# A gated network's second output product: four products per period against a seven-product scheme over six periods

## The chip, the cores and the metric

One core of one Trainium2 chip runs the whole kernel. The metric is the device time of one execution in microseconds (us); a kernel's time is the median of several runs. All inputs and outputs are float32.

## What is computed

```python
qn = q / (norm(q, axis=1) + 1e-6); kn = k / (norm(k, axis=1) + 1e-6)
a = softmax(kn.T @ qn / tau)              # 256 x 256, channels by channels
x = v @ a                                 # 6016 tokens x 256
xn = x / sqrt(mean(x*x) + 1e-6) * rms_g   # first gated layer
x = (silu(xn @ w_gate) * (xn @ w_val)) @ w_out
out = (sigmoid(x @ w_gate2) * (x @ w_val2)) @ w_out2   # second gated layer, d_ff = 1536
```

## The kernel before

Every operand of a matmul is held as a high and a low part (h and l, float32r), and each product is three matmuls, `mm3` (L104): high by high, high by low, low by high. Activations lie transposed: 256 channels are two chunks of 128 partitions, tokens are the columns. The 47 tiles of 128 tokens form 12 blocks, and two blocks one of six pairs; a pair has two halves of 512 columns (pair 2, which comes last in the second layer, has halves of 448). The 1536 hidden channels are 12 groups f of 128.

A head computes the attention and x. Then the first two pairs of layer one run block by block (`plain_gv`, `plain_h`, `out_mm`), while the weights of both layers are converted in steps that the loop pumps (`conversion`, L123): seven operands of 128 x 128 for gate and value and two output weights per f, split in high and low. Those of layer one stay in SBUF, those of layer two go to DRAM (`w2d`, L213) and are loaded once, f by f, into the buffers of layer one's weights during layer two's first pair (L850).

The rest is a stream of periods, one per (layer, pair, f), 48 of layer one and 72 of layer two. `period` (L491) is written out by hand, and every engine executes its instructions in that order. For gate and value it uses a scheme of seven products (`product`, L484) in place of eight on the two halves and two channel chunks of a pair: Z, B, then the fourth product of the previous period (T4), T2 into Z, B21 into A, T3 into Z, S4 into B; ScalarE and VectorE copy and add between them. The banks "g" (Z, B) and "v" (A, D) have two buffers each. In the same period the previous period's hidden values of both halves are finished (sigmoid on g1, `v1 = v1 * g1`, `v0 = v0 * sg0`) and split into hh and hl (L526, L527, L541, L542), and four output products (`out_mm`, L455) of the period before that add into four PSUM banks, y0, y1, at0, at1: two behind the A product, two at the end. After 12 periods the four banks are copied out and stored (`evacuate`, L468). `slots` holds per period what else is placed at its points "early", "ACT", "DVE", "end": the load of the next pair's operands, three sums on POOL (and a fourth later), and their splits. POOL does nothing else in layer two; all DMAs are issued from SP.

After the last period only the rest of its hidden values, four output products and the copies are left.

## Time and profile before

| | us |
|---|---|
| median of 3 runs | 1215.25 (1211.85 to 1217.26) |
| the profiled execution | 1211.54 |
| its span | 1209.8 |
| TensorE busy | 1179.6 (5398 matmuls) |
| VectorE / ScalarE / POOL busy | 781.7 / 792.6 / 180.2 |

Busy time is the union of an engine's rows; the rows of matmuls and of ScalarE and VectorE instructions overlap, so a row's duration is longer than the distance at which the next one can start. The first 100 us are the attention, the weights are converted up to about 300 us, the stream of layer one ends and that of layer two begins at about 655 us.

### The profile page before, as it was taken

Reading aid. Unit: us, or ns where it says so; the run is one execution under the profiler, and the core shown is the slowest. Engines: PE = TensorE matmul, PEld = TensorE weight load, DVE = VectorE, ACT = ScalarE, POOL = GpSimd, SP = SyncE. Lnnn points to the kernel's source line nnn. Section 1 sums busy time; section 2 is a strip of 40 time slices with the busy share of each in tenths; the row PEclk is TensorE's granted clock in tenths of the full one; section 3 lists DMA queues with packets and bytes.
Section 4 is the critical chain, followed back from the end, with each engine's and each line's share of the span. In section 5 each row is a group of like instructions: output and inputs, shape, how many; then the busy total and the mean of one; then the engine's idle time right before and its main releaser. Section 6 shows DMA issues by size and latency. Waiting matters only on the chain.

```text
span 1209.8 us, 14740 instructions
## 1 busy us (share of the span) xinstructions
PE 1179.6 (98%) x5398; PEld 987.9 (82%) x5398; DVE 781.7 (65%) x1166; ACT 792.6 (66%) x1459; POOL 180.2 (15%) x207
## 2 busy tenths in 40 slices
PE   8898989999999999999999999999999999999997
PEld 7786767788899888888888788888888888888997
DVE  6898888886556556556556556556555565565554
ACT  7766667775466666666666666666666666666664
POOL 0133665553200100100100100100100100100000
PEclk9999999999999999999999999999999999999999
DMA  9662335765300200200344400200200200100000
GB/s 345 242 231 105 122 107 188 269 223 211 112 1 1 66 1 1 70 1 1 130 162 162 156 1 1 70 1 1 70 1 1 70 1 1 66 1 1 35 1 31
DMA packets 42473, 98.48 MB, mean 81 GB/s; under 512 B 4768, under 2 KB 14496, under 8 KB 42400
## 3 DMA queue, kind: packets, MB, share of 16 engines
q1 hardware_dynamic: 42256, 97.41, 23.0%
q8 instruction: 42, 0.69, 0.2%
q14 instruction: 31, 0.25, 0.1%
q10 hardware_dynamic: 144, 0.13, 0.0%
HBM read 64.36 MB, written 33.16 MB: 81 GB/s over the span
## 4 chain that ended last, share of the span: by engine, by line
PE 79%; DVE 1%; ACT 1%; issue 0%; POOL 0%; ACTq 0%; DVEq 0%
PE g L105 12%; PE g L107 12%; PE g L106 12%; PE v L105 5%; PE v L106 5%; PE v L107 5%; PE at L106 5%; PE at L107 5%; PE at L105 5%; PE y L105 5%; PE y L106 5%; PE y L107 5%; DVE hl L527 0%; DVE v L521 0%; ACT hh L526 0%
## 5 line engine op out<-in xcount | busy, mean ns | idle before, releaser
L520 ACT ACTIVATE g<-g 128x512 f32<-128x512 f32 (+1 forms) x120 | 74.6, 621 | 158.9 <-DVE g L558 158.9
L556 DVE TENSOR_TENSOR v<-g,e 128x512 f32<-128x512 f32 (+1 forms) x120 | 81.4, 678 | 128.6 <-ACT v L554 128.6
L521 DVE TENSOR_TENSOR v<-v,g 128x512 f32<-128x512 f32 (+1 forms) x120 | 84.8, 707 | 81.9 <-ACT g L520 81.9
L527 DVE TENSOR_TENSOR hl<-v,hh 128x512 fp32r<-128x512 f32 (+1 forms) x120 | 83.3, 694 | 81.1 <-ACT hh L526 81.1
L542 DVE TENSOR_TENSOR hl<-v,hh 128x512 fp32r<-128x512 f32 (+1 forms) x120 | 81.4, 678 | 70.9 <-ACT hh L541 70.3
L554 ACT COPY v<-g 128x512 f32<-128x512 f32 (+1 forms) x120 | 67.2, 560 | 83.9 <-PE g L107 83.1
L105 PE MATMUL g<-xh,wh 128*128 128x512 f32 (+1 forms) x300 | 115.5, 385 | 0.2
L107 PE MATMUL g<-xh,wl 128*128 128x512 f32 (+1 forms) x300 | 115.3, 384 | 0.0
L106 PE MATMUL g<-xl,wh 128*128 128x512 f32 (+1 forms) x300 | 115.3, 384 | 0.0
L105 PE MATMUL at<-hh,wh 128*128 128x512 f32 (+1 forms) x288 | 111.2, 386 | 1.9 <-ACT hh L526 1.3
L105 PE MATMUL g<-qh,wh 128*128 128x512 f32 (+1 forms) x276 | 107.9, 391 | 5.2 <-ACT wh L182 5.2
L106 PE MATMUL at<-hl,wh 128*128 128x512 f32 (+1 forms) x288 | 111.5, 387 | 0.6 <-DVE hl L527 0.6
L107 PE MATMUL at<-hh,wl 128*128 128x512 f32 (+1 forms) x288 | 110.9, 385 | 0.0
L105 PE MATMUL y<-hh,wh 128*128 128x512 f32 (+1 forms) x288 | 110.9, 385 | 0.0
L106 PE MATMUL y<-hl,wh 128*128 128x512 f32 (+1 forms) x288 | 110.9, 385 | 0.0
L107 PE MATMUL y<-hh,wl 128*128 128x512 f32 (+1 forms) x288 | 110.9, 385 | 0.0
L107 PE MATMUL g<-qh,wl 128*128 128x512 f32 (+1 forms) x276 | 107.8, 390 | 2.2 <-DVE wl L190 2.2
L106 PE MATMUL g<-ql,wh 128*128 128x512 f32 (+1 forms) x276 | 107.0, 388 | 0.0
L105 PE MATMUL v<-qh,wh 128*128 128x512 f32 (+1 forms) x216 | 85.3, 395 | 3.9 <-DVE hl L451 3.6
L538 ACT COPY g<-g 128x512 f32<-128x512 f32 (+1 forms) x120 | 69.5, 579 | 28.3 <-PE g L107 28.0
L106 PE MATMUL v<-ql,wh 128*128 128x512 f32 (+1 forms) x216 | 83.9, 388 | 0.0
L107 PE MATMUL v<-qh,wl 128*128 128x512 f32 (+1 forms) x216 | 83.8, 388 | 0.0
(160 smaller groups left out, 2754.7 us busy)
## 6 DMA issues: line engine op xcount, KB each, us to landing
wraw<-in_w_dram SPq DMA_DIRECT2D x24, 768.0 KB, 4.9
w2d<-w2h SPq DMA_DIRECT2D x12, 576.0 KB, 2.8
w2d<-w2l SPq DMA_DIRECT2D x12, 576.0 KB, 3.2
wh<-w2d SPq DMA_DIRECT2D x12, 576.0 KB, 3.7
wl<-w2d SPq DMA_DIRECT2D x12, 576.0 KB, 4.7
vraw<-in_v_t_dram SPq DMA_DIRECT2D x11, 512.0 KB, 3.9
yd<-yo SPq DMA_DIRECT2D x20, 256.0 KB, 2.4
out_t_dram<-yo SPq DMA_DIRECT2D x20, 256.0 KB, 2.2
```

The source lines that it names most:

```text
L105: nc.tensor.matmul(ps, sh, mh, start=start, stop=False, skip_group_check=more)
L106: nc.tensor.matmul(ps, sh, ml, start=False, stop=False, skip_group_check=more)
L107: nc.tensor.matmul(ps, sl, mh, start=False, stop=stop, skip_group_check=more)
L520: nc.scalar.activation(out=pv["g1"], in_=pv["g1"], func=(AF.Silu, AF.Sigmoid)[pl])
L521: nc.vector.tensor_mul(pv["v1"], pv["v1"], pv["g1"])
L527: nc.vector.tensor_sub(hl1[:, :pw], pv["v1"], f32(hh1[:, :pw]))
L538: nc.scalar.copy(s["g1"], Z)
L542: nc.vector.tensor_sub(hl0[:, :pw], pv["v0"], f32(hh0[:, :pw]))
L554: nc.scalar.copy(D, Z)
L556: nc.vector.tensor_add(s["v1"], Z, e5)
```

## The change

Layer two's output product gets a scheme of seven products too. It pairs two groups f (hidden channels) and both output chunks, with the two halves of the columns; six periods' hidden values make three such pairs, a team, and a team has 7 kinds of operand times 3 pairs, 21 products. They run during the six periods that follow (`out_product`: one early in even periods, one behind the A product, two at the end), the last team's behind the last period. Two teams make a column pair. The sums of hidden values that the kinds need are made in place: a first sum and some third sums on VectorE, the others by DMAs from POOL's queue that add one SBUF tile into another (`more`), nine products ahead of their use. Signs are put into the gating multiplications (`gated`). The hidden tiles are kept in float32 in buffers of layer one's weights, and split when their product comes near (`split_high`, `split_low`). Results are gathered from four banks Z, B, A, D into four SBUF tiles after each kind (`gather`, called by `flush`) and stored from them.

Layer two's gate and value weights are now reloaded from DRAM for each period into three buffers (`gw_load`), and the output operands for each kind into four (`ow_load`). The output weights go to DRAM unsplit during conversion, and are loaded, split, summed and stored in layer one's stream (`out_load` to `sums_low`). The order of the operands in a weight tile changes; layer one's v1 gets one buffer instead of two; a_h and a_l move into a weight buffer. Not shown below: those moves, and the halved slices in `conversion`.

```diff
     NQ = 9
-    A11, A12, A21, A22, OUT, S1, S2, S4 = 0, 1, 2, 3, 4, 6, 7, 8
+    S1, S2, S4, A11, A12, A21, A22, OUT = range(8)
     S3 = A21
...
-    w2d = [dram.tile([P, 2, NQ, P], F32, name=f"w2d{f}") for f in range(NF)]
+    gd = [dram.tile([P, 2, NG, P], F32, name=f"gd{f}") for f in range(NF)]
+    rd = [dram.tile([P, 4, P], F32, name=f"rd{i}") for i in range(NF // 2)]
+    od = [dram.tile([P, 8, 2, NJ, P], F32, name=f"od{g}") for g in range(2)]
...
             t = w["t"]
+            if l:
+                nc.sync.dma_start(out=rd[f // 2][:, f % 2 * 2 : f % 2 * 2 + 2], in_=t[:, OUT:])
...
+    stream0 = [(0, p, f) for p in range(PLAIN, NP) for f in range(NF)]
+    stream1 = [(1, p, f) for p in (0, 1, 3, 4, 5, 2) for f in range(NF)]
+    stream = stream0 + stream1
+    HALF = NF // 2
+    teams = [(p, g) for _, p, f in stream1[::NF] for g in range(2)]
+    gw = {}
+    def gw_load(n):
+        if n < len(stream1):
+            gw[stream1[n]] = [wp.tile([P, NG, P], F32R, tag=f"w{e}{n % 3}", name="gw") for e in "hl"]
+            for e, t in enumerate(gw[stream1[n]]):
+                nc.sync.dma_start(out=f32(t), in_=gd[stream1[n][2]][:, e])
     def product(ps, it, i, a, start, stop=True):
         l, p, f = it
         h, lo = ops[l, p][i]
         w = hw[p]
-        mm3(ps[:, :w], wh[l, f][:, a], wl[l, f][:, a], h[:, :w], lo[:, :w], start, stop, not start)
-    def period(it, pv, outs, last=False):
+        ch, cl = gw[it] if l else (wh[0, f], wl[0, f])
+        mm3(ps[:, :w], ch[:, a], cl[:, a], h[:, :w], lo[:, :w], start, stop, not start)
+    odd = {}
+    def out_load(i):
+        odd["t"] = sp.tile([P, 4, P], F32, tag="t1", name="ot")
+        nc.sync.dma_start(out=odd["t"], in_=rd[i])
+    def out_store(i, h, lo, first):
+        g, j = divmod(i, NJ)
+        for e, t in enumerate((h, lo)):
+            nc.sync.dma_start(out=od[g][:, first : first + 4, e, j], in_=f32(t))
+    def out_split(i):
+        odd["h"] = sp.tile([P, 4, P], F32R, tag="t2", name="oh")
+        nc.scalar.copy(odd["h"], odd["t"])
+    def out_low(i):
+        lo = sp.tile([P, 4, P], F32R, tag="ol", name="ol")
+        nc.vector.tensor_sub(lo, odd["t"], f32(odd["h"]))
+        out_store(i, odd["h"], lo, 0)
+    def out_sums(i):
+        w11, w21, w12, w22 = (odd["t"][:, u] for u in range(4))
+        nc.gpsimd.tensor_add(w22, w21, w22)
+        nc.gpsimd.tensor_sub(w21, w11, w21)
+        nc.gpsimd.tensor_sub(w11, w22, w11)
+        nc.gpsimd.tensor_sub(w12, w11, w12)
+    def sums_low(i):
+        lo = sp.tile([P, 4, P], F32R, tag="ol", name="ol")
+        nc.vector.tensor_sub(lo, odd["t"], f32(odd["h"]))
+        out_store(i, odd["h"], lo, 4)
+    homes = [f"w{e}{f}" for f in range(5, NF - 1) for e in "hl"]
+    hs, xs = [], []
+    def h_tile():
+        hs.append(wp.tile([P, 2, 512], F32, tag=homes[len(hs) % len(homes)], name="hs"))
+        return hs[-1]
+    def gated(out, v, gate, negative):
+        if negative:
+            nc.vector.scalar_tensor_tensor(out=out, in0=v, scalar=-1.0, in1=gate, op0=ALU.mult, op1=ALU.mult)
+        else:
+            nc.vector.tensor_mul(out, v, gate)
+    def first_sum(n):
+        w = hw[stream1[n][1]]
+        xs.append(sp.tile([P, 512], F32, tag=f"t{len(xs) % NJ}", name="t"))
+        nc.vector.tensor_add(xs[-1][:, :w], hs[n][:, 0, :w], hs[n][:, 1, :w])
+    def third_sum(n):
+        w = hw[stream1[n][1]]
+        b, d = hs[n - 1][:, 1, :w], hs[n][:, 1, :w]
+        if n % HALF == HALF - 1:
+            nc.vector.tensor_add(b, b, d)
+        else:
+            more(b, d)
+    def more(to, t):
+        nc.gpsimd.dma_start(out=to, in_=t, accum_op=ALU.add)
+    KINDS = ("11", "S1", "12", "S2", "S4", "S3", "22")
+    PLACE = ("11", "21", "12", "22", "S2", "S3", "S4", "S1")
+    ow = deque()
+    ow_n = [0]
+    def ow_load():
+        i, k = divmod(ow_n[0], len(KINDS))
+        if i < len(teams):
+            tag = ("wh3", "wl3", "wh4", "wl4")[ow_n[0] % 4]
+            t = wp.tile([P, 2, NJ, P], F32R, tag=tag, name="ow")
+            nc.sync.dma_start(out=f32(t), in_=od[teams[i][1]][:, PLACE.index(KINDS[k])])
+            ow.append(t)
+        ow_n[0] += 1
+    job, kept = {}, {}
+    due, lows = deque(), deque()
+    LAST = len(KINDS) * NJ
+    def team_start(i):
+        p, g = teams[i]
+        w = hw[p]
+        if g == 0:
+            kept["r"] = [
+                t[:, e, :w] for t in (wp.tile([P, 2, 512], F32, tag=f"w{u}{NF - 1}", name="r") for u in "hl")
+                for e in range(2)
+            ]
+            kept["A"], kept["D"] = y_bank(1), at_bank(1)
+        n = HALF * i
+        job.clear()
+        job.update(
+            p=p, g=g, w=w, split=0, done=0, parts={},
+            x=NJ * i,
+            h=[[hs[n + 2 * j + u][:, e, :w] for u in range(2) for e in range(2)] for j in range(NJ)],
+            A=kept["A"][:, :w], D=kept["D"][:, :w], r=kept["r"],
+        )
+    def split_high(ahead):
+        while job and job["split"] < min(LAST, job["done"] + ahead):
+            i = job["split"]
+            k, j = divmod(i, NJ)
+            a, b, c, d = job["h"][j]
+            src = xs[job["x"] + j][:, : job["w"]] if KINDS[k] == "S1" else {"12": c, "S4": d, "S3": b}.get(KINDS[k], a)
+            h, lo = (hidden(t)[:, : job["w"]] for t in ("hh", "hl"))
+            nc.scalar.copy(h, src)
+            job["parts"][i] = h, lo
+            job["split"] += 1
+            lows.append((i, h, lo, src))
+    def split_low():
+        while lows:
+            i, h, lo, src = lows.popleft()
+            nc.vector.tensor_sub(lo, src, f32(h))
+            k, j = divmod(i, NJ)
+            a, b, c, d = job["h"][j]
+            if KINDS[k] in ("11", "S2"):
+                more(a, b if KINDS[k] == "11" else c)
+    def out_product():
+        if not job or job["done"] == LAST:
+            return
+        k, j = divmod(job["done"], NJ)
+        kind = KINDS[k]
+        w = job["w"]
+        if j == 0 and kind in ("11", "S1"):
+            name = "Z" if kind == "11" else "B"
+            job[name] = (y_bank if kind == "11" else at_bank)(0)[:, :w]
+        ps = job[{"12": "A", "22": "D", "S1": "B", "S4": "B"}.get(kind, "Z")]
+        start = j == 0 and (kind in ("11", "S1") or (job["g"] == 0 and kind in ("12", "22")))
+        mm3(ps, ow[0][:, 0, j], ow[0][:, 1, j], *job["parts"].pop(job["done"]), start, True, not start)
+        job["done"] += 1
+        if j == NJ - 1:
+            ow.popleft()
+            ow_load()
+            due.append(partial(gather, kind, dict(job)))
+    def send(v, c, e, t):
+        p, w = v["p"], v["w"]
+        nc.sync.dma_start(out=out_t[c * P : (c + 1) * P, p0[p] + e * w : p0[p] + (e + 1) * w], in_=t)
+    def minus(out, src):
+        nc.scalar.activation(out=out, in_=src, func=AF.Copy, scale=-1.0)
+    def gather(kind, v):
+        Z, B, A, D = (v.get(n) for n in "ZBAD")
+        r11, r12, r21, r22 = v["r"]
+        add, sub = nc.vector.tensor_add, nc.vector.tensor_sub
+        again = v["g"]
+        if kind in ("11", "S2", "S3"):
+            r = {"11": r11, "S2": r12, "S3": r21}[kind]
+            if again:
+                add(r, Z, r)
+            else:
+                nc.scalar.copy(r, Z)
+        if kind == "S1":
+            if again:
+                sub(r22, r22, B)
+            else:
+                minus(r22, B)
+        if kind == "S3":
+            add(r22, Z, r22)
+        if kind == "S4":
+            sub(r12, r12, B)
+        if again and kind in ("12", "22"):
+            r, ps = (r11, A) if kind == "12" else (r21, D)
+            sub(r, r, ps)
+        if again:
+            for k, c, e, r in (("12", 0, 0, r11), ("S4", 0, 1, r12), ("S3", 1, 1, r22), ("22", 1, 0, r21)):
+                if k == kind:
+                    send(v, c, e, r)
+    def flush():
+        while due:
+            due.popleft()()
+    def period(it, pv, n, outs=()):
...
             product(s["v0"], s["it"], T4, A22, False)
-            nc.vector.tensor_mul(s["v0"], s["v0"], s["sg0"])
+            gated(s["h"][:, 0, :w] if l else s["v0"], s["v0"], s["sg0"], l and f % 2)
+        def split(ahead):
+            if n1 >= 0:
+                split_high(ahead)
+                split_low()
+        def out(count):
+            for _ in range(count):
+                if outs:
+                    outs.popleft()()
+                elif n1 >= 0:
+                    out_product()
         if it:
             l, p, f = it
...
             pl, pp, pf = pv["it"]
             pw = hw[pp]
             nc.scalar.activation(out=pv["g1"], in_=pv["g1"], func=(AF.Silu, AF.Sigmoid)[pl])
-            nc.vector.tensor_mul(pv["v1"], pv["v1"], pv["g1"])
-        if it:
-            nc.scalar.copy(A, Z)
-        if pv:
+            gated(pv["v1"], pv["v1"], pv["g1"], pl and pf % 2 == 0)
+        flush()
+        if n1 > 0 and n1 % HALF == 0:
+            team_start(n1 // HALF - 1)
+        if n1 > 0 and pf % 2:
+            third_sum(n1 - 1)
+        split(2)
+        if not it:
+            while job["done"] < LAST:
+                split(3)
+                out_product()
+                flush()
+            return
+        nc.scalar.copy(A, Z)
+        if pv and pl == 0:
             hh1, hl1 = hidden("hh"), hidden("hl")
             nc.scalar.copy(hh1[:, :pw], pv["v1"])
             nc.vector.tensor_sub(hl1[:, :pw], pv["v1"], f32(hh1[:, :pw]))
             hid[pl, pp, 1, pf] = hh1, hl1
-            if not pv.get("done"):
-                fourth(pv)
+            fourth(pv)
+        e5 = sp.tile([P, 512], F32, tag="e5", name="e5")[:, :w]
+        if pv and pl:
+            nc.scalar.copy(e5, B)
+            if n1 > 0:
+                split_high(3)
+            fourth(pv)
+            gw_load(n1 + 2)
+            split_low()
+            if pf % 2 == 0:
+                first_sum(n1 - 1)
         at("early")
-        if it:
-            e5 = sp.tile([P, 512], F32, tag="e5", name="e5")[:, :w]
+        if not (pv and pl):
             nc.scalar.copy(e5, B)
-            product(Z, it, T2, S2, False)
-            product(A, it, B21, A12, False)
-            s["g1"] = sp2.tile([P, 512], F32, tag="g1", name="g1")[:, :w]
-            nc.scalar.copy(s["g1"], Z)
-        if pv:
+        else:
+            out(1 if n1 % 2 == 0 else 0)
+        product(Z, it, T2, S2, False)
+        product(A, it, B21, A12, False)
+        s["g1"] = sp2.tile([P, 512], F32, tag="g1", name="g1")[:, :w]
+        nc.scalar.copy(s["g1"], Z)
+        if pv and pl == 0:
             hh0, hl0 = hidden("hh"), hidden("hl")
             nc.scalar.copy(hh0[:, :pw], pv["v0"])
             nc.vector.tensor_sub(hl0[:, :pw], pv["v0"], f32(hh0[:, :pw]))
             hid[pl, pp, 0, pf] = hh0, hl0
-        if it:
-            s["sg0"] = ip2.tile([P, 512], F32, tag="sg", name="sg")[:, :w]
-            nc.scalar.activation(out=s["sg0"], in_=A, func=act)
-        for _ in range(2):
-            outs.popleft()()
-        at("ACT")
-        at("DVE")
-        if it:
-            product(Z, it, T3, S3, False)
-            D = s["v0"] = gv_bank("v")[:, :w]
-            nc.scalar.copy(D, Z)
-            s["v1"] = sp2.tile([P, 512], F32, tag="v1", name="v1")[:, :w]
-            nc.vector.tensor_add(s["v1"], Z, e5)
-            product(B, it, B22, S4, False)
-            nc.vector.tensor_add(s["g1"], s["g1"], B)
-        if last:
-            outs.popleft()()
+        flush()
+        if n1 % 2 == 0:
+            split(3)
+        if n1 >= 0:
+            out(2 if outs else 1)
+            at("DVE")
+        s["sg0"] = ip2.tile([P, 512], F32, tag="sg", name="sg")[:, :w]
+        nc.scalar.activation(out=s["sg0"], in_=A, func=act)
+        if n1 < 0:
+            out(2)
+            at("ACT")
+            at("DVE")
+        product(Z, it, T3, S3, False)
+        D = s["v0"] = gv_bank("v")[:, :w]
+        nc.scalar.copy(D, Z)
+        if l:
+            s["h"] = h_tile()
+            s["v1"] = s["h"][:, 1, :w]
+        else:
+            s["v1"] = sp.tile([P, 512], F32, tag="t0", name="v1")[:, :w]
+        nc.vector.tensor_add(s["v1"], Z, e5)
+        flush()
+        if n1 >= 0:
+            split_high(3)
+            at("ACT")
+        product(B, it, B22, S4, False)
+        nc.vector.tensor_add(s["g1"], s["g1"], B)
+        split_low()
+        if n == len(stream) - 1:
+            out(2)
             fourth(s)
-            s["done"] = True
-        while outs:
-            outs.popleft()()
+        else:
+            out(max(2, len(outs)))
         at("end")
         return s
...
-            s = period(it, pv, outs, n == len(stream) - 1)
+            if 6 <= n < 6 + 6 * NF // 2 and n % NF % 6 == 0:
+                i = n // 6 - 1
+                slots[0].setdefault("end", []).append(partial(out_load, i))
+                slots[1].setdefault("ACT", []).append(partial(out_split, i))
+                slots[1].setdefault("end", []).append(partial(out_low, i))
+                slots[2].setdefault("end", []).append(partial(out_sums, i))
+                slots[4].setdefault("ACT", []).append(partial(out_split, i))
+                slots[4].setdefault("end", []).append(partial(sums_low, i))
+            s = period(it, pv, n, outs)
             if pv and pv["it"][:2] == (0, NP - 1):
                 g = pv["it"][2]
-                for d, e, tag in ((wh, 0, "wh"), (wl, 1, "wl")):
-                    d[1, g] = wp.tile([P, NQ, P], F32R, tag=f"{tag}{g}", name=tag)
-                    nc.sync.dma_start(out=f32(d[1, g]), in_=w2d[g][:, e])
+                if g < 3:
+                    gw_load(g)
+                if g == 4:
+                    for _ in range(4):
+                        ow_load()
             pv = s
-            outs = [(l, p, e, f) for e in (1, 0)]
-        for e in range(2):
-            for c in range(KC):
-                evacuate(*stream[-1][:2], e, c, c, e == 1)
+            outs = [(*it[:2], e, it[2]) for e in (1, 0)] if it and it[0] == 0 else []
```

## Rows read from the trace of the kernel before

**Rows 1.** The page's head: span; busy time, share and instructions by engine.

```profile
span 1209.8 us, 14740 instructions
PE 1179.6 (98%) x5398; PEld 987.9 (82%) x5398; DVE 781.7 (65%) x1166; ACT 792.6 (66%) x1459; POOL 180.2 (15%) x207
```

**Rows 2.** Stretches: length, busy time (x count) of each engine, PEclk, DMA share, GB/s.

```profile
190.00:220.00 30.00, 27.63 (x116) 21.01 (x114) 26.58 (x34) 21.13 (x38) 15.43 (x21) 1.00 0.62 219
655.00:1200.00 545.00, 544.66 (x2441) 457.67 (x2440) 320.29 (x492) 354.93 (x641) 25.56 (x20) 1.00 0.09 30
```

**Rows 3.** Timeline, a period of layer two, 512 columns: start, duration, instruction, [idle before].

```profile
899.77 0.39 PE L107 MATMUL g<-xh,wl 128*128 128x512 f32 x1
900.00 0.39 PE L105 MATMUL g<-xh,wh 128*128 128x512 f32 x1
...
900.25 0.57 ACT L554 COPY v<-g 128x512 f32<-128x512 f32 x1 [0.59 <-PE g L107]
...
900.86 0.69 DVE L556 TENSOR_TENSOR v<-g,e 128x512 f32<-128x512 f32 x1 [0.88 <-ACT v L554]
...
901.46 0.68 DVE L558 TENSOR_TENSOR g<-g,g 128x512 f32<-128x512 f32 x1
...
902.04 0.39 PE L105 MATMUL g<-xh,wh 128*128 128x512 f32 x1
...
902.17 0.63 ACT L520 ACTIVATE g<-g 128x512 f32<-128x512 f32 x1 [1.35 <-DVE g L558]
...
904.96 0.59 ACT L538 COPY g<-g 128x512 f32<-128x512 f32 x1 [0.29 <-PE g L107]
...
905.55 0.59 ACT L541 CAST hh<-v 128x512 fp32r<-128x512 f32 x1
...
906.03 0.61 ACT L546 ACTIVATE sg<-v 128x512 f32<-128x512 f32 x1
...
907.73 0.57 ACT L554 COPY v<-g 128x512 f32<-128x512 f32 x1 [0.59 <-PE g L107]
```

**Rows 4.** Timeline, the end of the kernel, 448 columns.

```profile
1190.69 0.36 PE L105 MATMUL g<-zh,wh 128*128 128x448 f32 x1
...
1197.37 0.37 PE L105 MATMUL g<-zh,wh 128*128 128x448 f32 x1
...
1197.78 0.36 PE L107 MATMUL g<-zh,wl 128*128 128x448 f32 x1
...
1201.84 0.62 DVE L527 TENSOR_TENSOR hl<-v,hh 128x448 fp32r<-128x448 f32 x1 [0.63 <-ACT hh L526]
...
1202.38 0.62 DVE L542 TENSOR_TENSOR hl<-v,hh 128x448 fp32r<-128x448 f32 x1
1202.52 0.47 PE L106 MATMUL at<-hl,wh 128*128 128x448 f32 x1 [0.19 <-DVE hl L527]
...
1205.08 1.86 SPq L480 DMA_DIRECT2D out_t_dram<-yo  x4
1205.47 0.54 ACT L473 COPY yo<-at 128x448 f32<-128x448 f32 x1
```

**Rows 5.** DMA issues: tiles, queue, count, KB each, median us to landing.

```profile
wl<-w2d SPq DMA_DIRECT2D x12, 576.0 KB, 4.7
...
yd<-yo SPq DMA_DIRECT2D x20, 256.0 KB, 2.4
...
in<-in_q_dram SPq DMA_DIRECT2D x13, 384.0 KB, 6.1
```

**Rows 6.** Timeline: VectorE beside POOL's pair sums.

```profile
686.74 1.78 DVE L527 TENSOR_TENSOR hl<-v,hh 128x512 fp32r<-128x512 f32 x1 [0.69 <-ACT hh L526]
...
864.74 1.29 POOL L392 TENSOR_TENSOR xs<-zl 128x512 f32<-128x512 f32 x1
...
865.44 1.14 DVE L521 TENSOR_TENSOR v<-v,g 128x512 f32<-128x512 f32 x1 [0.70 <-ACT g L520]
```

**Rows 7.** One tile's instructions: a conversion subtraction of layer two, duration min/median/max in ns.

```profile
L190 DVE TENSOR_TENSOR w2l<-wst,w2h x12: 947/1025/1215, 196.5 to 297.5; 128x768 fp32r<-128x768 f32 x12
```

More of the change, by code (lines that the diff above doesn't have):

```diff
@@ L194, in sums_high @@
             h = w["h"]
-            nc.scalar.copy(h[:, S1:], w["t"][:, S1:])
+            nc.scalar.copy(h[:, :A11], w["t"][:, :A11])
             if l:
@@ L279, in v_low, with x_mm @@
         vT[b].append(lo)
-    def x_mm(b, banks):
+    def x_mm(b, banks, a_h, a_l):
         h, lo = vT.pop(b)
@@ L680 @@
         nc.vector.tensor_copy(rq, rq_ps[:, :C])
+        a_h, a_l = (wp.tile([P, KC, C], F32R, tag=f"w{e}4", name="a") for e in "hl")
         low = small1.tile([P, KC], F32, name="low")
@@ L729 @@
                 load_v(blocks[n + 4])
-            x_mm(b, row_banks(n))
+            x_mm(b, row_banks(n), a_h, a_l)
             if n > 1:
@@ L763 @@
         assert len(at) == 2 * PLAIN * NF
-        stream = [(0, p, f) for p in range(PLAIN, NP) for f in range(NF)]
-        stream += [(1, p, f) for p in (0, 1, 3, 4, 5, 2) for f in range(NF)]
         hooks = {}
```

38 lines of the change are left out of this document (21 added, 17 removed).

## The prediction

> **What bounds the kernel now.** I read the head of the page and the table of stretches first [rows 1, 2]. The span is 1209.8 us, the profiled execution took 1211.5, and the runs' median of 1215.25 lies 3.7 above that; the sum below is made against 1211.5. In the stretch 655 to 1200 us, almost all of it the second layer, TensorE is busy 544.66 of 545 us at a granted clock of 1.00 (the level of 2.4 GHz), VectorE 59% and ScalarE 65%. So TensorE sets the pace there, and the next question is what one matmul costs. The duration of a row (0.39 us) is no price, since rows overlap: matmuls start 0.23 us apart, and a whole period of 33 matmuls lasts from one D copy to the next, 900.25 to 907.73, 7.48 us, or 0.2267 each [rows 3]. A product of three is then 0.68 us. For the last pair, 448 columns wide, the period is 1197.37 - 1190.69 = 6.68 us, 0.2025 a matmul [rows 4].
>
> The same rows give the latencies that the other engines need [rows 3]: a PSUM reader starts 0.25 us after the last matmul's issue slot (899.77 + 0.23 to 900.25); VectorE's v add starts after ScalarE's D copy (900.82 to 900.86); VectorE can start an instruction every 0.60 us, ScalarE every 0.48 (905.55 to 906.03), although one lasts 0.69 and 0.6; the sigmoid starts 0.13 after the next period's first matmul. TensorE starts 0.06 after VectorE's operand (1201.84 + 0.62 to 1202.52) [rows 4].
>
> **The change, part by part.**
>
> *Matmuls.* Each period keeps its 21 gate/value matmuls. Output products were four per period, and are now 21 per six periods: 63 matmuls for 72, in 12 teams, 108 fewer, 24.2 us of issue. An even period has 11 products (7.48 us, as before), an odd one 10 (6.80). That shortens the 27 odd periods of 6 to 59 by 27 x 0.68 = **18.4 us**. In the last pair 18 matmuls go (3.6 us), but its first six periods now carry the products of a 512-wide team (63 x 0.024 = 1.5 more, 0.3 of which was there before): **-2.4**.
>
> *Five periods without output products.* Team 0 starts in period 6, so periods 1 to 5 hold 21 matmuls, 4.76 us of issue, and lose their filling. From T3's end, D copy and v add end 0.25 + 0.57 + 0.04 + 0.69 = 1.55 us later; the next period's first product reuses that bank and has only S4 (0.68) ahead of it: it waits 0.93. The g1 copy (0.25 + 0.59 + 0.06 = 0.90 after T2) has one product before T3: 0.22. So 5.91 us instead of 7.48: **-7.85**, and period 6 begins with the same 0.93: **+0.9**.
>
> *Splits, sums and gathers.* Two hidden splits per period become 3.5, on ScalarE (copy) and VectorE (subtraction); VectorE gets 36 first sums and 12 third sums; the 24 evacuations become 84 gather operations (24 on ScalarE, 60 on VectorE). Per period of 7.14 us VectorE then has 4 gate and add instructions, 3.5 splits, 0.7 sums, 0.6 pair splits and 0.8 gathers, 9.6 at 0.60, 5.8 us (81%); ScalarE has 6, 3.5, 0.6 and 0.3, 10.4 at 0.48 to 0.52, 5.2 us (73%). Neither is the bound by load. By order, I laid the two periods out from these latencies (times from the period's first matmul). Sigmoid 0.13, gated v1 about 0.84, split copy 0.64, A copy 1.13 to 1.70, while T2 needs it at 2.04 (odd) or 2.72 (even): no wait. Splits are two to three products ahead. What falls out of that:
> - At a team's start nothing is split ahead. VectorE must do gated v1 (0.84), in half of the cases the gather of "22", the third sum, and only then the first subtraction, which ends at 2.75 or 3.36; product 0's second matmul would issue at 2.27. TensorE, with T2 and everything behind it, waits 0.54 or 1.15 us. Eleven starts lie in the stream: 5 x 1.15 + 5 x 0.54 + 0.98 for the first (its period starts early) = **+9.4**.
> - A gather on ScalarE ahead of the A copy in an odd period (two per team of the first half) moves it to 2.2: 0.22 each, 6 teams, 2.6. A gather on VectorE between v add and g1 add (kinds "12" and "S2" of the second half) delays the sigmoid by 0.6: 0.34 and 0.11, 5 teams, 2.3. Together **+4.9**.
>
> *The tail.* Before, the last copy ended 1205.47 + 0.54 = 1206.01, 8.0 us after the last T3's end (1197.78 + 0.20) [rows 4]. Now team 11's 21 products all stand behind the last period. From T3's end, S4, two products and the fourth take 2.43; gated h0 follows at 2.7, gated v1 and the third sum behind it, so the first subtraction ends at 4.9. From there VectorE has 21 subtractions and 8 gathers at 0.54 (1201.84 to 1202.38), and three buffers bind split i+3 to product i: some 2.16 us per kind against 1.82 of matmuls. The last product ends at 20.4, the last gather at 21.2. That is 13.2 later; one store instead of four at the end of SP's queue gives back 0.4: **+12.8**.
>
> *Accumulating DMAs.* 96 of 256 KB, from POOL's queue (before only the pair sums there, four per pair). No row shows one. Nearest are SP's 256 KB stores with 2.4 us to landing and the 384 KB loads in the crowded start with 6.1 [rows 5]. A sum has nine products to land: about 15 us in the stream, 5 us in the tail (issued at 4.9, its split due at 9.9), there twice in a row. Bounds: 0 (2.4 plus issue) and +10 (10 us, half as much again as the slowest row); three go together, so I take a little over the stores' time, about 5.5: **+1**. Behind a late one ScalarE's copy waits, and in order the A copy and TensorE. On POOL they stand in order with the pair sums, three of 1.3 us [rows 6] behind period 2 of each pair: some 4 us of the 15.
> The Trainium skill (DMA: Bandwidth & Descriptors, "Anatomy of one DMA") puts a transfer from the GpSimd path at about 2.0 us plus bytes over 436 GB/s, 2.6 us here as an estimate; by it this term is 0 and the sum 1211.
>
> *Queues and loads.* SP now issues two 448 KB loads each period instead of 24 of 576 KB once, and 84 of 384 KB; 576 KB land in 4.7 us [rows 5] and are used 1.7 periods (10 us or more) after issue, so 0; uncovered, 72 times up to 4.7. They wait for a fourth product just ahead in the order; behind them stand pair loads due a whole pair later. In layer one's stream six groups of one load, two copies, two subtractions, four POOL sums and four stores lie beside a TensorE without idle time: 0, and 24 x 0.6 = 14 at most if not covered. The second layer's conversions copy and subtract 512 elements for 768 (VectorE 1.0 us each, 12 of them [rows 7]) in a stretch where VectorE is busy 26.6 of 30 and TensorE 27.6 [rows 2]: between 0 and -3, I take **-0.7**, as only half of them meet idle TensorE. Buffers of a_h and v1 move: 0, their readers end long before.
>
> *VectorE beside POOL.* One gated product took 1.14 us instead of 0.69 while POOL's pair sum ran, a split 1.78 [rows 6]. The new VectorE work is mostly of that kind, and 24 pair sums lie in layer two. From 0 to 24 x 0.45 = 11; most meet slack: **+1**.
>
> **Sum:** -18.4 - 2.4 - 7.85 + 0.9 + 9.4 + 4.9 + 12.8 + 1 - 0.7 + 1 = +0.6, so 1211.5 becomes **1212 us**: the 24 us of issue saved come back as waits, half of them in the tail.
>
> **The rivals.**
> *The waits are filled (faster).* If the order leaves no wait at team starts and gathers, 14.3 us stay: 1212 - 14 = 1198; with half of them 1205. For it: TensorE waited nowhere for ScalarE or VectorE between 655 and 1200, with 40% slack. Against: the subtraction that product 0 needs cannot start before gated v1. 30%.
> *Accumulating DMAs are late (slower).* In the tail each microsecond over 5 costs two: 10 us to landing gives 1222, 12 us 1226. It decides from about 8 us on; over 15 us each of 11 teams would pay twice too, 1212 + 22 x the excess. For it: nothing shows their price, and three run together with the weight loads. Against: stores of the same size need 2.4. 16%.
> *VectorE is the bound (slower).* At 81% it no longer makes up what the pair sums take from it: if each of the 24 blocks it for 0.45 on the way to the sigmoid, where an odd period has 0.28 to spare, it is +11 for +1: 1222. For it the rows of 1.14 and 1.78; against, the 1.3 us left over in a period. 12%.
> The Trainium skill (SBUF — State Buffer, "Who interferes with whom") says that a VectorE instruction with two SBUF inputs and a GpSimd instruction that reads SBUF exclude each other; by that rule this rival's blocking is certain and only its cover is open, and the rows of 1.14 and 1.78 agree.
> *The matmuls do not go.* The diff plainly has 21 products for 24; no chance of its own.
>
> **How the numbers follow.** About 0.5% (6 us) is what a measurement of this kernel tells from no change. The forecast, 1206 to 1218, has 42%; faster by more 30%; slower by more 16 + 12 = 28%. The range takes in the full fill (1198, with -3 for conversions, 1196) and late DMAs up to 14 us or half of both slower cases (1230).
>
> **What would show it.** Right: 5290 matmuls; periods 1 to 5 at 5.9 us; odd periods near 6.8; a wait of TensorE on the subtraction at each team's start, 0.5 to 1.2 us; the last matmul some 20 us after the last T3. Wrong: TensorE waiting on accumulating DMAs, team starts without wait, or a tail much shorter than 20 us.

## The result, and the profile after

The changed kernel takes 1227.78 us in the median (1226.30 to 1228.99), the kernel before 1215.45 in the same comparison: a ratio of 1.0105 [1.0079, 1.0130], slower by 1%. The profiled execution took 1227.86 us with a span of 1225.8; the span is 16.0 longer than before. Between the medians lie 12.3 us, between the two profiled executions 16.3; 3.2 of those lie ahead of the stream, in a part that differs from execution to execution (last section). The forecast was 1212, no change; the time lies inside the range, on the side that had a chance of 28%.

The head of the page of the kernel after, and its row for 655 to 1200 us from the table of stretches (length, then busy time and count of PE, PEld, DVE, ACT, POOL, then PEclk, DMA share, GB/s), answering to [rows 1, 2]:

```profile
span 1225.8 us, 15986 instructions
PE 1178.7 (96%) x5290; PEld 966.1 (79%) x5290; DVE 911.7 (74%) x1382; ACT 847.5 (69%) x1591; POOL 281.1 (23%) x327
...
655.00:1200.00 545.00, 529.58 (x2302) 427.50 (x2301) 434.55 (x674) 400.71 (x749) 106.84 (x110) 1.00 0.82 235
```

The 108 matmuls are gone (5398 to 5290). But TensorE, which was idle for 0.3 us of these 545, is now idle for 15.4, at the same granted clock of 1.00; VectorE went from 59% to 80% busy. What ended the longest of these idle times is in the waits of the kernel after, 600 us to the end, for TensorE (us in total, times, longest):

```profile
PE y L108 <- DVE hl L626: 9.0, 14, 1.5
PE g L107 <- DVE hs L798: 6.8, 9, 0.9
...
PE g L107 <- DVE g L804: 0.9, 4, 0.2
```

The first is the forecast wait for a product's subtraction, at team starts and in the tail. The second is a bank of PSUM that the v add has not yet read. Five of the nine times lie in the first pair, the five forecast periods without output products; the four others, one in each of the next four pairs, belong to the term of VectorE beside POOL, which had 1 us for all of them together. The last line is the same four places once more, 1.2 us later, where the g1 add is late.

To place the time I compare the two traces at the D copies (ScalarE's copy of T3's bank, once a period, [rows 3]):

| stretch | before | after | difference |
|---|---|---|---|
| start to the first D copy of the stream | 323.39 | 326.58 | +3.2 |
| layer one's stream | 352.18 | 355.03 | +2.9 |
| layer two, first pair | 90.04 | 83.35 | -6.7 |
| second to fourth pair | 269.46 | 271.46 | +2.0 |
| fifth pair | 89.44 | 89.88 | +0.4 |
| last pair | 73.73 | 73.89 | +0.2 |
| last D copy to the end of the span | 11.56 | 25.61 | +14.05 |

So the tail costs what was forecast, and the pairs that should pay for it do not. The periods of a pair are counted from 0 to 11, and the distance behind a period is the one from its D copy to the next. These distances in a full pair (twelve periods) are 6.80, 7.48, 7.26, **9.22**, 6.80, **8.66**, 7.18, 7.48, 6.80, 7.48, 7.18, **8.18** us, 90.5 in all, against 12 x 7.48 = 89.8 before. The 4.08 us of matmuls that six odd periods save are there (6.80), and 4.8 us of stalls with them: 1.75 behind period 3, 1.18 and 0.70 at the two team starts, 0.38 twice and 0.46 at gathers.

The stall behind period 3, in the timeline of the kernel after (start, duration, engine, line, operation, tiles, [idle before and what ended it]):

```profile
782.62 0.86 POOL L571 DMA_DIRECT2D hs<-hs  x1 [2.43 <-DMA gw<-gd]
...
783.03 2.33 DVE L626 TENSOR_TENSOR hl<-hs,hh 128x512 fp32r<-128x512 f32 x1
...
783.18 1.62 POOL L398 TENSOR_TENSOR xs<-xl 128x512 f32<-128x512 f32 x1
...
784.88 1.64 POOL L398 TENSOR_TENSOR xs<-xl,xs 128x512 f32<-128x512 f32 x1
...
785.28 0.68 DVE L553 TENSOR_TENSOR hs<-v,sg 128x512 f32<-128x512 f32 x1
...
785.89 1.18 DVE L626 TENSOR_TENSOR hl<-hs,hh 128x512 fp32r<-128x512 f32 x1
...
786.48 0.57 ACT L792 COPY v<-g 128x512 f32<-128x512 f32 x1 [0.76 <-PE g L109]
786.49 1.75 POOL L398 TENSOR_TENSOR xs<-xl 128x512 f32<-128x512 f32 x1
...
787.00 1.78 DVE L559 TENSOR_TENSOR t<-hs 128x512 f32<-128x512 f32 x1
...
788.70 0.68 DVE L798 TENSOR_TENSOR hs<-g,e 128x512 f32<-128x512 f32 x1
...
789.43 0.50 PE L107 MATMUL g<-qh,gw 128*128 128x512 f32 x1 [0.95 <-DVE hs L798]
```

Three pair sums stand back to back on POOL, each 1.6 to 1.75 us (1.29 in [rows 6]), and the three VectorE instructions with both inputs in SBUF that meet them take 1.18 to 2.33 instead of 0.68. The gated v0 at 785.28, whose v lies in PSUM, takes 0.68 beside the second sum: not every VectorE instruction is held. The D copy ends at 787.05, the v add that should start then starts at 788.70, and TensorE waits for it. In the kernel before, the same pair's sums ran as soon as their loads had landed and their buffers were free, the first of them at 771.44:

```profile
771.44 1.30 POOL L392 TENSOR_TENSOR xs<-xl 128x512 f32<-128x512 f32 x1 [64.42 <-DMA xl<-yd]
```

Now they come in one period and without a gap: POOL works in order, and an accumulating DMA stands ahead of them after 2.43 us of waiting. In the next pair the same wait, of the same length, is put down to the subtraction in front of that DMA:

```profile
873.10 0.86 POOL L571 DMA_DIRECT2D hs<-hs  x1 [2.43 <-DVE hl L626]
```

That this DMA is what brings the three sums together is read from the order in the trace; no run moved it alone.

### The profile page after: what moved, and what is told of

Read it like the earlier page. It is cut to its first block, busy times and chain, and to the rows that moved or that the text cites. A ratio compares the mean times of both kernels' runs of the same rounds, so it can differ in the third digit from the quotient of the medians.

```text
span 1225.8 us, 15986 instructions
## 1 busy us (share of the span) xinstructions
PE 1178.7 (96%) x5290; PEld 966.1 (79%) x5290; DVE 911.7 (74%) x1382; ACT 847.5 (69%) x1591; POOL 281.1 (23%) x327
## 4 chain that ended last, share of the span: by engine, by line
PE 62%; DVE 11%; ACT 4%; issue 4%; DMA 1%; POOL 0%; SPq 0%; DVEq 0%; ACTq 0%; POOLq 0%
PE g L107 10%; PE g L108 9%; PE g L109 9%; PE v L107 4%; PE v L108 4%; PE y L108 4%; PE v L109 4%; PE y L109 4%; PE y L107 4%; PE at L108 3%; PE at L109 3%; PE at L107 3%; DVE hl L626 2%; DVE g L804 2%; ACT v L792 1%
## 5 line engine op out<-in xcount | busy, mean ns | idle before, releaser
L571 POOL DMA_DIRECT2D hs<-hs x96 | 83.6, 914 | 466.1 <-DVE hl L626 197.3
L626 DVE TENSOR_TENSOR hl<-hs,hh 128x512 fp32r<-128x512 f32 (+1 forms) x216 | 152.5, 714 | 20.5 <-ACT hh L618 19.7
L618 ACT CAST hh<-hs 128x512 fp32r<-128x512 f32 (+1 forms) x216 | 130.1, 609 | 4.6 <-PE y L109 1.4
L792 ACT COPY v<-g 128x512 f32<-128x512 f32 (+1 forms) x120 | 67.2, 560 | 65.8 <-PE g L109 65.1
L804 DVE TENSOR_TENSOR g<-g,g 128x512 f32<-128x512 f32 (+1 forms) x120 | 79.7, 664 | 0.0
L107 PE MATMUL g<-xh,gw 128*128 128x512 f32 x180 | 73.0, 405 | 5.7 <-DVE hs L798 4.9
L785 ACT ACTIVATE sg<-v 128x512 f32<-128x512 f32 (+1 forms) x120 | 71.1, 592 | 3.7
L107 PE MATMUL g<-qh,wh 128*128 128x512 f32 x168 | 66.8, 397 | 6.6 <-ACT wh L187 5.3
L747 ACT COPY v<-g 128x512 f32<-128x512 f32 (+1 forms) x120 | 68.0, 567 | 4.8 <-PE g L109 0.3
L108 PE MATMUL g<-xl,gw 128*128 128x512 f32 x180 | 70.3, 391 | 0.0
L109 PE MATMUL g<-xh,gw 128*128 128x512 f32 x180 | 70.2, 390 | 0.0
L751 DVE TENSOR_TENSOR hl<-v,hh 128x512 fp32r<-128x512 f32 (+1 forms) x48 | 32.7, 681 | 32.4 <-ACT hh L750 32.4
```

What stands on the lines that cost most here:

```text
L107: nc.tensor.matmul(ps, sh, mh, start=start, stop=False, skip_group_check=more)
L108: nc.tensor.matmul(ps, sh, ml, start=False, stop=False, skip_group_check=more)
L109: nc.tensor.matmul(ps, sl, mh, start=False, stop=stop, skip_group_check=more)
L571: nc.gpsimd.dma_start(out=to, in_=t, accum_op=ALU.add)
L618: nc.scalar.copy(h, src)
L626: nc.vector.tensor_sub(lo, src, f32(h))
```

## The experiments

The theory, ORDER in the expectations: the loss is no load and no bandwidth but places in the order of in-order engines, which are the pair sums on POOL's queue, the first operand of a team split too late, a ScalarE copy in front of which a load is late, and VectorE's sequence in the tail. Rivals: the sums' or the splits' sheer work (moving them gives nothing), traffic (DMA engines 82% busy, 9% before), and, for the tail, TWO LIMITS: VectorE and the accumulating DMAs stand at the same height, so that taking one away gives little. Edits are to the changed kernel; ratios are to the kernel before, and the changed kernel's own is 1.0105 [1.0079, 1.0130]. Some edits are shown shortened.

**Layer two's pair sums left out** (`pair_sum`):

```diff
+        if l:
+            sums[out] = ab[0]
+            return
```

> Changed kernel with the pair sums of layer two left out (an operand stands for its sum, so the output is another one); POOL then has only the accumulating DMAs there. Theory ORDER (VectorE in its order is what TensorE waits for, and three pair sums back to back block its two-input instructions in period 4 of each pair, 1.75 us above an even period): five pairs lose 1.75 to 2.4 us each, so about 1227.8 - 9 = 1219 us, and the D-copy distance behind period 3 falls from 9.2 to about 7.5. Theory DMA (accumulating DMAs and reloads, with the DMA engines 82% busy, are late): the sums carry nothing, 1227 to 1228, distance stays above 9.

1220.08 us, 1.0051 [1.0032, 1.0070]. The same place in its timeline (lines shifted by 3):

```profile
779.03 0.68 DVE L562 TENSOR_TENSOR t<-hs 128x512 f32<-128x512 f32 x1
...
780.48 0.57 ACT L795 COPY v<-g 128x512 f32<-128x512 f32 x1 [0.78 <-PE g L109]
...
781.08 0.69 DVE L801 TENSOR_TENSOR hs<-g,e 128x512 f32<-128x512 f32 x1 [1.37 <-ACT v L795]
...
788.11 0.57 ACT L795 COPY v<-g 128x512 f32<-128x512 f32 x1 [0.43 <-PE g L109]
```

The v add starts with the end of the copy, and the next D copy comes after 7.63 us instead of 9.24 (786.48 to 795.72). A full pair takes 88.9 us for 90.5: 1.6 us less in the second to fourth pair and 1.2 in the fifth make 6.0, and the ratio fell by 0.0054, 6.6 us. The blocking by the sums is shown, a little smaller than expected.

**Layer one's splits a period later** (shortened):

```diff
-slots[1] ACT out_split; slots[1] end out_low; slots[2] end out_sums; slots[4] ACT out_split; slots[4] end sums_low
+slots[2] ACT out_split; slots[2] end out_low; slots[3] end out_sums; slots[5] ACT out_split; slots[5] end sums_low
```

> Changed kernel with the six output-weight splits of layer one's stream moved one period later, away from their load. Theory ORDER: in periods 13, 25 and 37 ScalarE waits in order for a load that stands behind four operand loads on SP's queue, and the D copy behind it is late by 1.7, 0.6 and 0.6 us, with some 0.4 in the periods after: about 1227.8 - 3.4 = 1224.4, and these distances become 7.5. Rival: the evacuations of the same period make the wait (the kernel before has 7.35 to 7.6 there), nothing changes, 1228.

1224.38 us, 1.0080 [1.0062, 1.0097]. What stood in the way is in the timeline of the kernel after, behind period 12 of layer one:

```profile
408.74 0.57 ACT L792 COPY v<-g 128x512 f32<-128x512 f32 x1 [0.22 <-PE g L109]
...
409.24 2.11 SPq L358 DMA_DIRECT2D xl<-xd  x4
...
411.45 0.37 SPq L514 DMA_DIRECT2D ot<-rd  x1
...
417.44 0.62 ACT L523 CAST oh<-ot 128x512 fp32r<-128x512 f32 x1 [2.32 <-DMA ot<-rd]
417.96 0.58 ACT L792 COPY v<-g 128x512 f32<-128x512 f32 x1
```

The load of the output weights was issued behind four operand loads, ScalarE waited 2.32 us for it, and the D copy behind it came 9.22 us after the one before. This happened at the three groups where a pair's loads stand ahead (9.22, 8.07, 8.12). With the edit these three distances are 7.36, 7.48, 7.48, and the stream of layer one 352.45 us for 355.03 (354.9 to 356.4 in the seven profiles with this part as in the change; the medians alone, with overlapping intervals, would not tell the two kernels apart). Of the 3.1 us gained at the three places some came back in the next periods (8.01, 7.68, 7.73): in the kernel of this run POOL's pair sums of layer one met VectorE there, as these two of its rows show.

```profile
419.20 1.47 DVE L553 TENSOR_TENSOR v<-v,g 128x512 f32<-128x512 f32 x1 [0.70 <-ACT g L733]
...
420.08 1.75 POOL L398 TENSOR_TENSOR xs<-xl 128x512 f32<-128x512 f32 x1
```

**A team's first operand split at the end of the period before** (two new functions, `presplit` and `prelow`, do for product 0 what `split_high` and `split_low` do):

```diff
         if n1 >= 0:
             split_high(3)
+            if pre is not None:
+                presplit(pre)
             at("ACT")
         product(B, it, B22, S4, False)
         nc.vector.tensor_add(s["g1"], s["g1"], B)
         split_low()
+        if pre is not None:
+            prelow(pre)
```

> Changed kernel with the first operand of each team split at the end of the period before its team starts, ahead of the gated product, the gather and the third sum. Theory ORDER: the waits of TensorE on the subtraction at a team's start (0.7 and 1.2 us, 11 starts) go, and the tail starts its first product earlier: 1227.8 - 8 to -10, about 1219. Theory DMA: the first operand was not what the team waited for, 1227 to 1228.

1214.96 us, 1.0015 [1.0001, 1.0030]: 0.0090 or 11 us back, the largest gain of one edit. A team start in the kernel after, then in this one:

```profile
802.52 0.57 ACT L792 COPY v<-g 128x512 f32<-128x512 f32 x1 [0.76 <-PE g L109]
...
805.11 0.69 DVE L553 TENSOR_TENSOR hs<-hs,g 128x512 f32<-128x512 f32 x1 [0.70 <-ACT g L733]
805.72 0.68 DVE L680 TENSOR_TENSOR r<-r,at 128x512 f32<-128x512 f32 x1
806.32 0.69 DVE L566 TENSOR_TENSOR hs<-hs 128x512 f32<-128x512 f32 x1
806.92 1.29 DVE L626 TENSOR_TENSOR hl<-hs,hh 128x512 fp32r<-128x512 f32 x2
807.66 0.50 PE L108 MATMUL y<-hl,ow 128*128 128x512 f32 x1 [0.87 <-DVE hl L626]
...
811.17 0.57 ACT L792 COPY v<-g 128x512 f32<-128x512 f32 x1 [0.45 <-PE g L109]
```

```profile
802.88 0.57 ACT L808 COPY v<-g 128x512 f32<-128x512 f32 x1 [0.76 <-PE g L109]
...
804.69 0.69 DVE L603 TENSOR_TENSOR hl<-hs,hh 128x512 fp32r<-128x512 f32 x1
805.47 0.69 DVE L553 TENSOR_TENSOR hs<-hs,g 128x512 f32<-128x512 f32 x1
...
810.36 0.57 ACT L808 COPY v<-g 128x512 f32<-128x512 f32 x1 [0.43 <-PE g L109]
```

In the first, gated v1 (L553), a gather (L680) and the third sum (L566) stand ahead of the subtraction, and TensorE waits for it; in the second it stands ahead of them, and 8.65 becomes 7.48. The other team start, 8.17, becomes 7.48 too. No work was removed: order alone.

**The tail: the last team's gathers, its accumulating DMAs (first and second edit), and both left out (both edits).**

```diff
+        if v["x"] == NJ * (len(teams) - 1):
+            add = sub = lambda *args: None
```
```diff
-            if KINDS[k] in ("11", "S2"):
+            if KINDS[k] in ("11", "S2") and job["x"] != NJ * (len(teams) - 1):
```

> Changed kernel with the last team's eight gather operations on VectorE left out (its results are stored without them). Theory ORDER: the tail runs at VectorE's pace, 21 subtractions and 8 gathers at 0.54 us, so about 7 x 0.54 = 3.8 us go, 1224. Theory DMA: the tail waits for accumulating DMAs (6.7 us to landing, twice in a row) and keeps its 25.6 us from the last D copy to the end, at most 1 us less for the last gather: 1227.

> Changed kernel with the last team's six accumulating DMAs (of 11 and S2) left out. The run without the gathers kept its tail: ScalarE then waited 4.1 us for accumulating DMAs. Theory TWO LIMITS (VectorE's subtractions and gathers, and the DMAs, end at about the same time in the tail): this run alone brings 0 to 1.5 us, with VectorE still there; from the last D copy to the end 24 to 25.6 us. Theory DMA ALONE: 3 to 4 us less, the tail 21.5 to 22.5.

> Changed kernel with both the last team's gather operations on VectorE and its accumulating DMAs left out. Theory TWO LIMITS: now both limits are gone, the tail falls by 3.5 to 5 us, to about 21, bound by the three buffers of split operands (two products of three cost about as much as their splits). Rival (the buffers alone set the tail): still 25.

The tail (last D copy to the end of the span) is 25.61 us with the change, 27.15 without the gathers (1226.34 us, 1.0105 [1.0085, 1.0125]), 23.9 without the DMAs (1224.82, 1.0095 [1.0073, 1.0117]), and 19.64 without both (1221.89, 1.0072 [1.0051, 1.0094]). The intervals of the three times overlap that of the change, so the stretch has to decide; in four profiles with the change's tail it lies between 25.6 and 26.3. ORDER alone had VectorE's sequence as the tail's limit and misses with the gathers. Without the DMAs 1.7 us go, a little more than TWO LIMITS expected; without both 6.0 go, more than its 3.5 to 5. The 4.3 us between these two are what eight gathers at 0.54 cost, so that VectorE and the DMAs limit the tail at nearly the same height, and the buffers alone (still 25) do not. The waits of the tail name the DMAs; the row of the kernel after, then that of the kernel without gathers:

```profile
ACT hh L618 <- DMA hs<-hs: 1.1, 2, 0.6
```

```profile
ACT hh L618 <- DMA hs<-hs: 4.1, 3, 1.6
...
PE at L107 <- ACT hh L618: 1.8, 3, 0.8
```

With VectorE out of the way, ScalarE waits three times for a sum's DMA, and TensorE for ScalarE. But that run changed one thing more. The four stores of the result no longer follow their gathers, and all go out together, at the time of the last sums; the stores of the kernel after, then of the kernel without gathers:

```profile
1213.33 9.99 SPq L652 DMA_DIRECT2D out_t_dram<-r  x4
```

```profile
1211.20 2.76 SPq L652 DMA_DIRECT2D out_t_dram<-r  x4
```

From the last accumulating DMA's start to the end of the wait for it 8.1 us pass there (1212.98 to 1221.11), against 5.7 in the median for 224 KB with the change. How much of the 4.1 us is due to the stores is not separated; the two limits rest on the other two runs.

**Layer two's pair sums on VectorE, in periods 1 and 2** (shortened; `one_sum` does one of the sums of `pair_sums`):

```diff
-        nc.gpsimd.tensor_sub(t, *ab)
+        (nc.vector if l else nc.gpsimd).tensor_sub(t, *ab)
...
-slots[2] end pair_sums
+slots[1] DVE one_sum(T1, T3, B11); slots[2] DVE one_sum(T2, B22, T1); slots[2] end one_sum(T3, B22, T3)
```

> Changed kernel with layer two's pair sums on VectorE, spread over periods 1 and 2 of each pair (the fourth where it was), nothing left out. Theory ORDER: they no longer run on POOL beside VectorE; the distance behind period 3 falls from 9.2 to about 7.6 as without the sums, and 24 instructions of 0.6 us find a place beside TensorE: 6 to 8 us less, ratio to the kernel before about 1.005. Rival (VectorE is full): what is saved in period 4 comes back in periods 1 to 3, ratio 1.010.

1227.57 us, 1.0113 [1.0090, 1.0137]: nothing gained. Behind period 3 the distance is 7.67, as hoped, but behind period 1 it is now 8.0 to 9.1:

```profile
773.83 0.69 DVE L398 TENSOR_TENSOR xs<-xl 128x512 f32<-128x512 f32 x1 [2.18 <-DMA xl<-yd]
774.44 0.68 DVE L803 TENSOR_TENSOR hs<-g,e 128x512 f32<-128x512 f32 x1
...
775.18 0.50 PE L107 MATMUL g<-qh,gw 128*128 128x512 f32 x1 [1.00 <-DVE hs L803]
```

VectorE, in order, waits 2.18 us for the operand's load, and the v add behind it holds TensorE. The sum takes 0.69 us here, where POOL's had lengthened the instructions beside it. The ratio is still the one that the rival, a full VectorE, had given; whether it is fullness or place, the run with the sums in periods 2, 3, 5 and 6 decides, below.

**The last three edits' kinds together** (layer one's splits later, first operands ahead, sums as just now):

> Changed kernel with all three: output-weight splits one period later, the first operand of a team split ahead, pair sums of layer two on VectorE. By theory ORDER the gains add, as they lie in different periods: 1226 - 2 to 3 - 11 - 6 to 8, about 1205 to 1207, ratio to the kernel before 0.993 to 0.995. If VectorE is full (the rival), two of them get in each other's way at the ends of the periods: 0.998 to 1.002.

1213.89 us, 1.0006 [0.9991, 1.0022]; the hoped-for 1205 to 1207 missed, and the rival's ratio met. The distances behind period 1 show the same wait (7.62 in the first pair, 8.4 to 9.1 in three, 11.43 in one).

**The same with the sums on VectorE in periods 2, 3, 5 and 6**, when the loads have landed (shortened):

```diff
+for i, x in ((2, (T1, T3, B11)), (3, (T3, B22, T3)), (5, (T2, B22, T1)), (6, (T4, B21, T2))):
+    slots[i].setdefault("DVE", []).append(partial(one_sum, *nxt, *x))
```

> As the run with all three, but the four pair sums of layer two stand on VectorE in periods 2, 3, 5 and 6 of each pair, one each, behind their loads. Theory ORDER: the run with all three lost 1.0 to 4.6 us per pair behind period 1, where the first sum waited on VectorE for its load with everything behind it; that goes, some 1.6 us a pair and 3 more in one pair, so 1213.9 - 8, about 1206, ratio to the kernel before 0.993 to 0.996. Rival (VectorE is full, the place does not matter): the wait comes back in the new periods, ratio 1.000.

1205.28 us, 0.9943 [0.9920, 0.9965]; a full pair takes 87.6 us. Same work, another place: 7.6 us less than the run before, and the rival that VectorE is full falls with it.

**Gathers behind the copy that TensorE needs**: `flush()` ahead of the A copy moves behind the B copy, and the one behind the v add moves behind the g1 add.

> As that, with the gathers moved in the order: behind the A copy and the e5 copy instead of ahead of them, and behind the g1 add instead of between v add and g1 add. Theory ORDER: the waits of 0.38 us behind periods 6 and 10 (ScalarE's gather ahead of the A copy in an odd period) and of 0.45 behind period 2 (VectorE's gather between the adds) go: 1.2 us a pair, about 6 to 7 us, ratio 0.988 to 0.991. Rival: the gathers only move the wait to another place, no change.

1202.24 us, 0.9903 [0.9878, 0.9928]; a full pair takes 86.1, against 12 x 7.14 = 85.7 without any wait. The interval overlaps a little that of the run before; the distances carry the reading: those behind periods 2, 6 and 10 of the third pair were 7.27, 7.46 and 7.16 and are 6.80, 7.01 and 6.79.

**The last team's first three operands split ahead of its last gating**:

> As that, with all three first operands of the last team split before the last period's gating. Theory ORDER: the tail's first wait of TensorE (1.5 us on the second subtraction) goes and the accumulating DMAs start 1 to 2 us earlier: 1 to 2 us less from the last D copy to the end, ratio 0.987 to 0.990. Theory TWO LIMITS, buffers included: only the start moves and the rest of the tail absorbs it, below 0.5 us.

1199.24 us, 0.9888 [0.9867, 0.9908], an interval that overlaps that of the run before it. The tail takes 24.9 for 24.97 and the full pairs are as before: nothing gained there, a miss for ORDER, although the ratio lies where it was expected. That is luck; the 3 us between the medians are no effect that the profiles show. TWO LIMITS had below 0.5 us, and in this tail ScalarE still waits 3.4 us, four times, for a sum's DMA.

**Layer one's pair sums on VectorE too**:

> As that, with layer one's pair sums on VectorE too (three pairs). Theory ORDER: behind period 13, 25 and 37 some 0.2 to 0.9 us are lost while POOL's sums block VectorE: 1 to 1.5 us less. Rival: the loads there are late and VectorE waits for them in order, up to 2 us more per pair.

**1195.71 us, 0.9866 [0.9844, 0.9889]**, 17 us faster than the kernel before. The head of its page and the stretch 655 to 1200:

```profile
span 1197.6 us, 15949 instructions
PE 1165.7 (97%) x5290; PEld 970.6 (81%) x5290; DVE 915.6 (76%) x1418; ACT 846.0 (71%) x1591; POOL 229.3 (19%) x291
...
655.00:1200.00 545.00, 532.09 (x2353) 439.00 (x2351) 446.41 (x724) 407.55 (x765) 83.03 (x96) 1.00 0.85 243
```

Layer one's pairs take 81.72, 89.63, 89.77 and 89.97 us for 82.21, 90.51, 89.87 and 89.97, 1.5 less, as expected; the interval of the times overlaps that of the run before. The span ends at 1197.6, so that these 545 us hold the whole tail, and the busy time of TensorE can't be set beside that of the other kernels; its 90.5 us of a full pair have become 86.1. VectorE does 36 instructions more than with the change (1418 for 1382) and holds little up by it: what is left above 85.7, some 0.4 us, lies behind periods 5 and 6 (7.7 and 7.0), where a sum and an operand's split stand on VectorE ahead of the v add. The DMA share is 0.85, higher than with the change: traffic was not what held it.

## Why the prediction was wrong

The sum ended at +0.6 us; the span grew by 16.0 and the time of the profiled executions by 16.3. The medians differ by 12.3, so that some 4 us of the miss belong to the two executions and not to the change (the bullet on the start). By the prediction's own steps:

- *Matmuls*: right. 5290, odd periods at 6.80 us.
- *Five periods without output products*: 6.05 to 6.09 us (four distances), forecast 5.91. With everything else of the first pair it gave -6.7, and the sum's terms for that pair come to about -7.0.
- *Team starts*: right, 1.18 and 0.70 for 1.15 and 0.54. The third experiment removed them with an edit of the order alone.
- *Gathers*: the mechanism right, 0.38 for 0.22 on ScalarE and 0.46 for 0.34 on VectorE. With the two points above they are what the last remainder below is put down to.
- *The tail*: +14.05, forecast +12.8 and +1. Right in size, in part by luck: I laid it out for VectorE alone, and the accumulating DMAs hold it at nearly the same height.
- *Accumulating DMAs*: 80 have 256 KB and 16 have 224, not 96 of 256. They need 6.7 us to land in the stream, where no compute engine waits for them, and 5.7 (224 KB) in the last pair and the tail, forecast 5.5; leaving out the tail's gave 1.7 us. The rival that they are late did not come about.
- *VectorE beside POOL, +1*: **the step that failed most.** It measured 6.0 us, 1.6, 1.6, 1.6 and 1.2 in four pairs. I had both prices in hand [rows 6] and spread them over VectorE's slack; I did not lay POOL's own order out, where the three sums now stand behind an accumulating DMA and fall into one period. The Trainium skill (SBUF — State Buffer, "Who interferes with whom") says that a VectorE instruction with two SBUF inputs contends with a GpSimd instruction that reads SBUF; the rows of 1.62 to 1.75 and 1.18 to 2.33 agree. The rival that I gave 12% has this mechanism, at 11 us.
- *Queues and loads, layer one's splits, 0*: **failed too**, +2.9 us (bound 14). I had the cover right, a TensorE without idle time, but not that the load stands in SP's queue behind four others and that ScalarE's D copy stands behind the split. The second experiment took 2.6 of it back.
- *Conversions, -0.7, and the start*: the first D copy came 3.2 us later instead of 0.7 earlier. This goes with the execution rather than the change: in five later profiles with the changed start and a mean granted clock of 1.00 over the first 60 us, as in the kernel before, it comes 0.8 to 2.6 us earlier than before; see the last section.

The distance from 1212.1 to 1227.86 is 15.8: 5.0 for the sums, 2.9 for layer one, 3.9 for the start and conversions, 0.3 each for the tail and what lies around the span, and the remaining 3.4 are put down to the small stalls of periods 1 to 5, team starts and gathers. Of the forecast as a whole, the balance of 24 us saved and 24 given back was drawn with two stalls missing. The rival "the waits are filled" does not hold for this kernel; its 14 us are near what it takes to order it, with the pair sums moved to VectorE: that kernel is 17 us faster than before.

What stays open: whether the tail could be shortened in a kernel that leaves nothing out, by moving both limits. That was not tried.

## What to carry to other kernels

Lay out the order of every in-order engine and queue period by period, POOL's and SP's too: the first operand of a new group is to be split ahead of the period that uses it, gathers go behind the copy that TensorE waits for, and an instruction that waits for a load goes where the load has landed. Price a blocked instruction at the place where it falls, not as a mean; two-input sums on POOL beside a dense VectorE cost more here (1.6 us a pair) than the same sums on VectorE in a good place (at most 0.4). A scheme whose last group stands behind the stream pays its whole chain of latencies there, here 14 of the 24 us that it saves.

## What the runs showed of the hardware

An accumulating DMA of 256 KB took 6.7 us in the median from issue to landing. In the same run plain stores of that size took 2.9 in layer one's part and 4.7 in layer two, where the DMA share is 0.82 (tiles, queue, count, KB, median us, kernel after):

```profile
hs<-hs POOLq DMA_DIRECT2D x80, 256.0 KB, 6.7
...
yd<-yo SPq DMA_DIRECT2D x20, 256.0 KB, 2.9
out_t_dram<-r SPq DMA_DIRECT2D x20, 256.0 KB, 4.7
...
hs<-hs POOLq DMA_DIRECT2D x16, 224.0 KB, 5.7
```

The 2.6 us that the prediction worked out from the Trainium skill (DMA: Bandwidth & Descriptors, "Anatomy of one DMA") does not hold for them here; the measurement decides. How much of the 6.7 is the adding and how much the traffic beside it, no run separates.

Behind period 3, beside POOL's sums of SBUF tiles, a VectorE instruction with two SBUF inputs took 1.18 to 2.33 us, and one with an input in PSUM 0.68 as ever.

Taking VectorE's gathers out of the tail did not shorten it (27.15 us for 25.6 to 26.3): its stores then ran beside the accumulating DMAs.

Before the stream begins, the same instructions do not always run at the same clock. The stretch 0 to 60 us of the kernel before, of the changed one, and of the run with the last team's operands ahead (length, busy times, PEclk, DMA share, GB/s):

```profile
0.00:60.00 60.00, 52.73 (x263) 45.67 (x264) 44.56 (x56) 43.84 (x73) 6.49 (x16) 1.00 0.79 296
```

```profile
0.00:60.00 60.00, 52.51 (x227) 44.69 (x228) 41.59 (x49) 40.51 (x62) 3.52 (x11) 0.94 0.79 290
```

```profile
0.00:60.00 60.00, 52.63 (x258) 44.96 (x259) 43.91 (x56) 43.38 (x72) 6.42 (x16) 1.00 0.80 296
```

The mean granted clock there is 1.00 or 0.94 in these three, with the second fewer matmuls are through by 60 us (227 for 263), and the first D copy of the stream comes at 323.4, 326.6 and 320.8 us. Over all 14 profiles it lies between 320.8 and 323.4 where that mean is 1.00 (six) and between 323.1 and 327.6 where it is 0.94 to 0.97 (eight). Spans of single profiles differ by as much, and the readings above therefore go from D copy to D copy.
